# Layer 2's first 256 columns in one part, and attention's buffers in one pool in the order in which they come free

## The chip, the cores and the metric

One NeuronCore of a Trainium2 chip runs the program. The metric is the device time of one execution in microseconds (us); lower is better.

## What is computed

Linear attention with a feature map, and on its output a soft mixture of experts. Shapes: q, k, v are 8 batches x 8 heads x 576 tokens x 64; the feature map has 128 features; the tokens x are 4608 x 512; there are 8 experts with 4 slots each, of width 1024. All is float32.

```python
def phi(x):
    proj = np.einsum('bhsd,df->bhsf', x, w_phi)
    proj = proj - np.max(np.abs(proj), axis=-1, keepdims=True)
    return np.concatenate([np.exp(proj), np.exp(-proj)], axis=-1)
q_p, k_p = (phi(q), phi(k))
kv = np.einsum('bhsf,bhsd->bhfd', k_p, v)
z = np.sum(k_p, axis=2)
num = np.einsum('bhsf,bhfd->bhsd', q_p, kv)
den = np.einsum('bhsf,bhf->bhs', q_p, z)[..., None] + 1e-06
...
logits = x @ phi                                   # 4608 x 32
d = softmax(logits, over tokens); slot_input = d.T @ x
slot_out[e] = np.maximum(slot_input[e] @ w1[e], 0.0) @ w2[e]
c = softmax(logits, over slots); out = c @ slot_out
```

## The kernel before

**Stages.** Attention runs in a pipeline over blocks of four tiles of 128 tokens. A planner (`Plan`) holds tasks by kind, each with what must have been done before it; `ORDER`, a string with one letter a task, says in which order they are recorded, and so in which order each engine finds its instructions. Two letters matter here: `I` (late), the load of one weight, and `Q` (close), the closing of a pool of attention's buffers. After attention come the token softmax and the slots' inputs (acc), then layer 1 (`layer1`, L930: si times w1 into hp), `hidden` (relu on ACT, a 32 x 32 transpose on DVE, giving sh), layer 2 (`layer2`, L995) and the outputs.

**Weights.** There are 64 loads (tiles wt0 to wt63) of 512 KB on SP's queue: 32 of w1, then 16 for the first 256 columns of w2 (wt32 to wt47), then 16 for the last 256 (wt48 to wt63). On chip they lie in 53 slots of 4096 bytes a partition. Slots 0 to 29 are free from the start. Slots 30 to 52 (`LATE`) lie where attention's buffers lie: a load into one waits until the users of those buffers (`over(j)`) are done: vt and vs (values), kf and qf (features of k and q), kvs, un, xs, xT, xc, xn and wk. The last 11 loads go into slots whose w1 part layer 1 has read. A load also waits for the landing of the one five before it, and SP takes its queue strictly in order. The buffers lie in six pools (`LAYOUT`, `LIFO`: x, v, q, u, t, c), and a pool's slots can be loaded once this pool is closed.

**Layer 2 and outputs.** `layer2(q, e)` multiplies the hidden values of expert e by 128 columns (`COLS`) of w2: eight matmuls of 32 rows, in four column slices that run side by side; a part q is complete after eight of these, and there are four parts. Then `slots(q)` copies it from PSUM (yp) to yt on DVE, `slots2(q)` sums the four slices and repeats them with `rep` on PE (psy) and copies that on ACT, and `outputs(q, g)`, three per part, multiplies by c (four pso matmuls of 384 columns), copies with DVE and ACT and issues two output DMAs of 384 KB on SP. `TAIL` orders this: L a call of `layer2`, s `slots`, r `slots2`, O `outputs`, P the second `hidden`.

```python
TAIL = "LPLLLLLLLLsrLLOLOLLLLsOrLLLOLLOLLLsOLrLLOLLOLLLsOrOOO"
```

All 24 outputs stand behind the last weight on SP. PE finds its instructions in the order of `TAIL`, and so do DVE and ACT.

Of the kernel before, what the change touches and what calls it, by code (L numbers as in the profile page):

```python
# [22 lines left out]
NCH = NT // CH  # L23
# [26 lines left out]
BASE, TOP = 8064, 226816  # L50
LAYOUT = (("x", "xs", (4096,) * 3, 1), ("v", "vt", (2624,) * 2, 0), ("v", "kf", (4096,) * 3, 0), ("v", "vs", (2624,) * 2, 0), ("q", "wd", (512,), 0),
          ("q", "qf", (4096,) * 3, 0), ("q", "kvs", (1056,) * 2, 0), ("u", "un", (2368,) * 2, 0), ("t", "xT", (4096,) * 3, 0), ("t", "wk", (4096,), 0),
          ("c", "xc", (8192,), 0), ("c", "xn", (8192,), 0), ("c", "xc", (8192,), 1))
LIFO = "xvqutc"


def regions():

    at, got = TOP - sum(sum(n) for _, _, n, _ in LAYOUT), []
    for k, name, sizes, first in LAYOUT:  # L60
        for i, n in enumerate(sizes):
            got.append((at, at + n, k, (name, (i + first) % max(len(sizes), first + 1))))
            at += n
    return got
# [4 lines left out]
PAD = REGIONS[0][0] - BASE - 4096 * FIRST  # L69
NSLOT = [FIRST] + [(max(b for _, b, x, _ in REGIONS if x == k) - BASE - PAD) // 4096 for k in LIFO]  # L70


def over(j):

    a = BASE + PAD + 4096 * j
    return [name for lo, hi, _, name in REGIONS if lo < a + 4096 and a < hi]

# [4 lines left out]
class Plan:  # L82
# [56 lines left out]
    "jAAknoowacwydfgccqhodgmmjfhillablsmpqzirrdktvrnjjfmkowvgjavwwAccbsxnyzofAhhrAAxdknilltviwmmrrjmgjvJpAqsrwfkAnhkx"  # L139
    "mnvooowdgtvwrvwcdccQMNikndjjlloIIIyzgjmmAAAfflrvhprimwhygjrzimqspQIIIIkknAAltRSRnSRoovIqrvTTRRwwvwAknrrrQIIyszST"  # L140
    "SSIItvAAwyvwUvTTzyzoAARRRSSXwyTTzSTY4AXRZYZSA0>UXQIRXYYSTTZWW002225536W36>553557799>QIII88868+8QIIW+++/=/=IIIIIO"
    "OP<!!!POP!")

COLS = 128
TAIL = "LPLLLLLLLLsrLLOLOLLLLsOrLLLOLLOLLLsOLrLLOLLOLLLsOrOOO"


@with_exitstack  # L150
def tile_kernel(ctx: ExitStack, tc, xT, vv, w, phi, phi4, w1, w2, cst, out):
# [24 lines left out]

    def pool(k, name, **kw):
        return stacks[k].enter_context(tc.tile_pool(name=name, **kw))

    area = {k: pool(k, k + "p", bufs=1, side="right") for k in reversed(LIFO)}  # L180

    def place_in(name, i, shape, as_=None):

        k = next(k for k, n, *_ in LAYOUT if n == name)
        return area[k].tile(shape, F32, tag=f"{name}{i}", name=as_ or name)

    for lo, hi, _, (name, i) in REGIONS:
        place_in(name, i, [128, (hi - lo) // 4], "lay")
# [687 lines left out]

    def close(k):
        stacks[k].close()
# [3 lines left out]
    every = {"x": [("proj", NB)], "v": [("kpos_exp", NB - 1), ("kvmm", len(pieces) - 1), ("vals", len(pieces) - 1), ("kvcopy", NU - 1)], "q": [("num", NK - 1)],  # L882
             "u": [("divide", (NU - 1, 2))], "t": [("zlog", c) for c in range(NCH)] + [("zcw", c) for c in range(NCH)] + [("zdt", c) for c in range(NCH)], "c": [("zsum", 4)]}
    users = {("xs", 1): [("proj", NB - 3)], ("xs", 2): [("proj", NB - 1)], ("xs", 0): [("proj", NB)], ("wd", 0): [("proj", NB)]}
# [59 lines left out]

    for i, k in enumerate(LIFO):
        add("close", i, None, 0.0, lambda k=k: close(k), after=every[k] + ([("close", i - 1)] if i else [("weight", FIRST - 1)]))
    for i, j in enumerate(LATE):
        add("late", i, SP, 1.3, lambda: load_w(1), after=[x for name in over(j) for x in users[name]], order=[("close", sum(j >= n for n in NSLOT) - 1)])
    with tc.manual_schedule(engines={SP, PE, ACT, DVE, POOL}):
# [39 lines left out]

        def layer2(q, e):  # L990
            if q not in yp:
                yp[q] = numbered(hb[0][q % 2], [128, COLS], "yp")
            for c in range(FC):
                g, o = 32 * (c % 4), c % 4 * DH + q % 2 * COLS
                nc.tensor.matmul(yp[q][g:g + 32], sh[e // 4][:, FC * (e % 4) + c],  # L995
                                 wt[NE * KC + (q // 2 * NE + e) * 2 + c // 4][:, o:o + COLS],
                                 start=(e == 0 and c < 4), stop=(e == NE - 1 and c >= 4), skip_group_check=True)

        yt = slot(spare[2], "yt").rearrange("p (i q c) -> p i q c", i=2, q=4)

        def slots(q):
            nc.vector.tensor_copy(yt[:, 0, q], yp[q])

        def slots2(q):
            ps = bank([128, COLS], "psy")
            for j in range(4):
                nc.tensor.matmul(ps[32 * j:32 * j + 32], rep, yt[:, 0, q], start=True, stop=True, skip_group_check=True)
            return nc.scalar.copy(yt[:, 1, q], ps).ins

        def outputs(q, g):  # L1010

            ps = [bank([128, TRI * 128], "pso") for _ in range(G)]
            c = ct[g // 2][:, g % 2 * TRI * 128:(g % 2 + 1) * TRI * 128]
            for j in range(G):
                rows = slice(32 * j, 32 * j + 32)
                nc.tensor.matmul(ps[j], yt[rows, 1, q], c[rows], start=True, stop=True)  # L1016
# [12 lines left out]
        cturn(1, 6, 9)  # L1029
        l2 = iter([(q, e) for q in range(4) for e in range(NE)])  # L1030
        done, outs = 0, []
        for step in TAIL:
            if step == "L":
                layer2(*next(l2))
            elif step == "P":
                hidden(1)
                cps += hb[1]
            elif step == "O":
                outputs(*outs.pop(0))
            elif step == "s":  # L1040
# [47 lines left out]
```

## Time and profile before

| | us |
|---|---|
| three timed runs | 309.3, 311.18, 311.4 (median 311.18) |
| the profiled execution's own time | 310.53 |
| its span, first to last instruction | 308.6 |
| around the span | 1.9 |

The profiled execution is one run. Its durations make up the working; its own time is 0.65 us under the median of the timed runs, which lie 2.1 us apart. PE is TensorE, DVE VectorE, ACT ScalarE, POOL GpSimd, and SPq the queue of SyncE, which issues the loads and outputs. A float32 matmul shows as two records on PE and two weight loads on PEld.

### The profile page before, as it was taken

Reading aid. Unit: us, or ns where it says so; the run is one execution under the profiler, and the core shown is the slowest. Engines: PE = TensorE matmul, PEld = TensorE weight load, DVE = VectorE, ACT = ScalarE, POOL = GpSimd, SP = SyncE. Lnnn points to the kernel's source line nnn. Section 1 sums busy time; section 2 is a strip of 40 time slices with the busy share of each in tenths; the row PEclk is TensorE's granted clock in tenths of the full one; section 3 lists DMA queues with packets and bytes.
Section 4 is the critical chain, followed back from the end, with each engine's and each line's share of the span. In section 5 each row is a group of like instructions: output and inputs, shape, how many; then the busy total and the mean of one; then the engine's idle time right before and its main releaser. Section 6 shows DMA issues by size and latency. Waiting matters only on the chain.

```text
span 308.6 us, 16094 instructions
## 1 busy us (share of the span) xinstructions
PE 296.2 (96%) x6805; PEld 251.5 (82%) x6805; DVE 243.3 (79%) x703; ACT 223.9 (73%) x658; POOL 159.2 (52%) x333
## 2 busy tenths in 40 slices
PE   8999999999999999999999999999999999999880
PEld 4999999998879999988799999897998853376550
DVE  0689888999898999889988989689887958624361
ACT  3999799888597998967978888887987560223351
POOL 1548677874367676953577776546788302000000
PEclk9999999999999999999999999999999999999996
DMA  7646564653339188435779888268487999999897
GB/s 244 215 153 189 179 191 149 240 181 127 99 91 329 52 261 285 163 113 185 252 230 331 259 266 293 55 206 295 118 262 267 355 340 374 411 407 408 349 359 309
DMA packets 23398, 74.01 MB, mean 240 GB/s; under 512 B 2592, under 2 KB 2976, under 8 KB 23328
## 3 DMA queue, kind: packets, MB, share of 16 engines
q1 hardware_dynamic: 23184, 72.94, 68.3%
q8 instruction: 53, 0.87, 1.1%
q14 instruction: 17, 0.14, 0.1%
q10 hardware_dynamic: 144, 0.07, 0.1%
HBM read 63.55 MB, written 9.44 MB: 237 GB/s over the span
## 4 chain that ended last, share of the span: by engine, by line
PE 90%; DVE 4%; issue 2%; DMA 1%; ACT 1%; POOL 0%; DVEq 0%; ACTq 0%
PE kvp L363 24%; PE psn L416 21%; PE psk L317 15%; PE psq L315 7%; PE yp L995 5%; PE hp L930 4%; PE pso L1016 3%; PE psq L496 3%; PE pss L556 2%; DMA wd<-w 1%; PE psw L229 1%; PE pss L659 1%; PE psk L309 1%; DVE un L432 1%; PE psl L506 1%
## 5 line engine op out<-in xcount | busy, mean ns | idle before, releaser
L336 POOL TENSOR_TENSOR vs<-vt,call 128x520 f32<-128x520 f32 (+3 forms) x128 | 91.2, 732 | 40.0 <-ACT call L325 17.8
L363 PE MATMUL kvp<-vs,kf 128*64 128x65 f32 (+1 forms) x2304 | 86.6, 229 | 0.1
L363 PEld LDWEIGHTS kvp<-vs,kf 128*64 128x64 f32 x2304 | 79.1, 138 | 5.4 <-issue 1.5
L416 PE MATMUL psn<-kvs,qf 128*64 128x65 f32 x2304 | 78.1, 222 | 0.2 <-issue 0.2
L416 PEld LDWEIGHTS psn<-kvs,qf 128*64 128x64 f32 x2304 | 72.7, 138 | 3.4 <-issue 1.3
L317 PE MATMUL psk<-wd,xs 64*128 64x128 f32 x560 | 70.9, 279 | 0.0
L315 PE MATMUL psq<-xs,wd 64*128 64x512 f32 x140 | 70.6, 616 | 0.4 <-PE psk L317 0.2
L317 PEld LDWEIGHTS psk<-wd,xs 64*128 64x128 f32 x560 | 63.9, 187 | 0.0
L321 DVE TENSOR_REDUCE call<-psk 128x4 f32<-128x512 f32 x72 | 47.6, 674 | 12.6 <-PE psk L309 5.9
L378 DVE TRANSPOSE_TENSOR_REDUCE call<-psq 128x16 f32<-128x512 f32 x72 | 48.9, 696 | 4.8 <-PE psk L317 4.1
L347 ACT ACTIVATE kf<-psk 128x512 f32<-128x512 f32 x72 | 42.1, 592 | 13.6 <-PE kvp L363 5.3
L462 POOL TENSOR_TENSOR xc<-un,dn 128x256 f32<-128x256 f32 x63 | 38.6, 616 | 14.3 <-DVE dn L447 9.9
L383 ACT ACTIVATE qf<-psq 128x512 f32<-128x512 f32 x72 | 42.0, 591 | 5.2 <-PE psk L317 2.4
L350 ACT ACTIVATE kf<-psk 128x512 f32<-128x512 f32 x72 | 42.4, 596 | 0.4 <-DVE call L321 0.4
L386 ACT ACTIVATE qf<-psq 128x512 f32<-128x512 f32 x72 | 42.4, 595 | 0.0
L427 DVE TENSOR_TENSOR un<-psn,eq 128x195 f32<-128x195 f32 x96 | 32.6, 348 | 6.4 <-PE psn L416 3.2
L432 DVE TENSOR_TENSOR un<-psn,un 128x195 f32<-128x195 f32 x96 | 32.2, 352 | 1.4
L394 ACT ACTIVATE call<-call 32x36 f32<-32x36 f32 x128 | 29.4, 229 | 5.0 <-DVE call L378 1.7
L400 DVE TENSOR_REDUCE eq<-call 32x9 f32<-32x36 f32 x128 | 25.9, 203 | 1.9 <-ACT call L394 0.6
L315 PEld LDWEIGHTS psq<-xs,wd 64*128 64x128 f32 x140 | 20.8, 186 | 5.7 <-issue 1.6
L1020 ACT COPY o<-pso 128x384 f32<-128x384 f32 x24 | 10.2, 484 | 15.3 <-PE pso L1016 15.3
L1020 DVE COPY o<-pso 128x384 f32<-128x384 f32 x24 | 12.1, 552 | 11.5 <-PE pso L1016 11.5
(125 smaller groups left out, 288.5 us busy)
## 6 DMA issues: line engine op xcount, KB each, us to landing
wt<-w SPq DMA_DIRECT2D x64, 512.0 KB, 6.2
xs<-xT SPq DMA_DIRECT2D x34, 512.0 KB, 4.8
vt<-vv SPq DMA_DIRECT2D x32, 325.0 KB, 3.1
out<-o SPq DMA_DIRECT2D x24, 384.0 KB, 3.9
xs<-xT SPq DMA_DIRECT2D x4, 256.0 KB, 3.9
phq<-phi SPq DMA_DIRECT2D x1, 256.0 KB, 2.7
cs<-cst SPq DMA_DIRECT2D x1, 81.0 KB, 3.4
wd<-w ACTq DMA_DIRECT2D x1, 64.0 KB, 3.0
```

Source lines behind the costliest of these rows:

```text
L315: nc.tensor.matmul(qx[b - 2], wd[qh], x[qh], start=True, stop=True)
L317: nc.tensor.matmul(kx[b][:, i], x[kh, i], wd[kh], start=True, stop=True)
L321: nc.vector.tensor_reduce(km[b][:, 2], kx[b], axis=AX, op=ALU.max, apply_absolute_value=True)
L336: nc.gpsimd.tensor_tensor(vs[b][:, :, place(b, u, t, o):place(b, u, t, o) + n], v[:, t + o:t + o + n].unsqueeze(1).broadcast_to([128, 2, n ...
L347: nc.scalar.activation(kf[b][:, 1], kx[b], AF.Exp, scale=-1.0)
L350: nc.scalar.activation(kf[b][:, 0], kx[b], AF.Exp)
L363: nc.tensor.matmul(ps[f:f + FE // 2, pn, o:o + m], kf[b][:, pn, NT * u + t - 4 * b, f:f + FE // 2], v2[:, pn, at:at + m], start=(t == 0 an ...
L378: nc.vector.tensor_reduce(mts.rearrange("p r j -> p j r")[:, o:o + 4], qx[b].rearrange("p j (r t) -> p (j r) t", t=32), axis=AX, op=ALU.ma ...
L383: nc.scalar.activation(qf[b][:, 0], qx[b], AF.Exp)
L386: nc.scalar.activation(qf[b][:, 1], qx[b], AF.Exp, scale=-1.0)
L416: nc.tensor.matmul(ps[64 * f:64 * f + 64, j, pn], q2[:, pn, 64 * f:64 * f + 64], kv[:, pn, b2], start=True, stop=True)
L462: (divider(u) if c == 2 else nc.gpsimd).tensor_tensor(x[:, :, h * D:(h + 1) * D], un[u][:, a:b, 0:64], dn[u][:, a:b].unsqueeze(2).broadcas ...
```

## The change

The buffers of attention go into one pool (`area`), closed once, and lie in a new order; all 23 late loads are recorded after this close (in `ORDER` the `I`s before it move behind it, the other letters keep their order). Each load still waits for the users of the buffers that its slot lies on. Layer 2 has three parts, of 256, 128 and 128 columns, in place of four of 128.

```diff
-LAYOUT = (("x", "xs", (4096,) * 3, 1), ("v", "vt", (2624,) * 2, 0), ("v", "kf", (4096,) * 3, 0), ("v", "vs", (2624,) * 2, 0), ("q", "wd", (512,), 0),
-          ("q", "qf", (4096,) * 3, 0), ("q", "kvs", (1056,) * 2, 0), ("u", "un", (2368,) * 2, 0), ("t", "xT", (4096,) * 3, 0), ("t", "wk", (4096,), 0),
-          ("c", "xc", (8192,), 0), ("c", "xn", (8192,), 0), ("c", "xc", (8192,), 1))
-LIFO = "xvqutc"
+LAYOUT = "xs1 vt0 xs2 xs0 wd0 kf0 kf1 vs0 vt1 kf2 vs1 kvs0 qf0 qf1 kvs1 qf2 un0 un1 xT0 xT1 xT2 xc0 wk0 xn0 xc1".split()
...
-COLS = 128
-TAIL = "LPLLLLLLLLsrLLOLOLLLLsOrLLLOLLOLLLsOLrLLOLLOLLLsOrOOO"
+PARTS = (0, 256), (256, 128), (384, 128)
+TAIL = "LLLPLLLLLsrLOLOLLLOLLOLLsOOLLrLOLLLLsOOrOOO"
...
-    area = {k: pool(k, k + "p", bufs=1, side="right") for k in reversed(LIFO)}
+    area = held.enter_context(tc.tile_pool(name="area", bufs=1, side="right"))
...
-    for i, k in enumerate(LIFO):
-        add("close", i, None, 0.0, lambda k=k: close(k), after=every[k] + ([("close", i - 1)] if i else [("weight", FIRST - 1)]))
+    add("close", 0, None, 0.0, close, after=sorted({x for name in users for x in users[name]} | {("kpos_exp", NB - 1), ("kvcopy", NU - 1), ("weight", FIRST - 1)}, key=str))
     for i, j in enumerate(LATE):
-        add("late", i, SP, 1.3, lambda: load_w(1), after=[x for name in over(j) for x in users[name]], order=[("close", sum(j >= n for n in NSLOT) - 1)])
+        add("late", i, SP, 1.3, lambda: load_w(1), after=[x for name in over(j) for x in users[name]], order=[("close", 0)])
...
-        def layer2(q, e):
-            if q not in yp:
-                yp[q] = numbered(hb[0][q % 2], [128, COLS], "yp")
+        def layer2(p, e):
+            at, n = PARTS[p]
+            if p not in yp:
+                yp[p] = numbered(hb[0][p % 2], [128, n], "yp")
             for c in range(FC):
...
-        def slots(q):
-            nc.vector.tensor_copy(yt[:, 0, q], yp[q])
+        def slots(p):
+            at, n = PARTS[p]
+            nc.vector.tensor_copy(yt[:, 0, at:at + n], yp[p])
...
-                nc.tensor.matmul(ps[32 * j:32 * j + 32], rep, yt[:, 0, q], start=True, stop=True, skip_group_check=True)
-            return nc.scalar.copy(yt[:, 1, q], ps).ins
+                nc.tensor.matmul(ps[32 * j:32 * j + 32], rep, yt[:, 0, at:at + n], start=True, stop=True, skip_group_check=True)
+            nc.scalar.copy(yt[:, 1, at:at + n], ps)
...
             else:
                 slots2(done)
-                outs += [(done, g) for g in range(3)]
+                at, n = PARTS[done]
+                outs += [(q, g) for q in range(at // 128, (at + n) // 128) for g in range(3)]
                 done += 1
```

On PE, around the end of layer 2's first part, the program before reads as follows. The numbers on wt are counters of the program: 5724 and 5726 are wt46 and wt47, 5216 to 5480 wt32 to wt38; x4 are the four slices.

```order
L995 MATMUL yp<-wt_5724,sh 32x128 x4
L995 MATMUL yp<-wt_5726,sh 32x128 x4
L995 MATMUL yp<-wt_5216,sh 32x128 x4
L995 MATMUL yp<-wt_5350,sh 32x128 x4
L1007 MATMUL psy<-yt,cs 32x128 x4
L995 MATMUL yp<-wt_5352,sh 32x128 x4
L995 MATMUL yp<-wt_5354,sh 32x128 x4
L995 MATMUL yp<-wt_5356,sh 32x128 x4
L995 MATMUL yp<-wt_5390,sh 32x128 x4
L1016 MATMUL pso<-ct,yt 128x384 x4
L995 MATMUL yp<-wt_5480,sh 32x128 x4
```

After the change the same place reads as follows; 5687 to 5691 are wt45 to wt47, 5723 to 5729 wt48 to wt51.

```order
L986 MATMUL yp<-wt_5687,sh 32x256 x4
L986 MATMUL yp<-wt_5689,sh 32x256 x4
L986 MATMUL yp<-wt_5691,sh 32x256 x4
L1000 MATMUL psy<-yt,cs 32x256 x4
L986 MATMUL yp<-wt_5723,sh 32x128 x4
L986 MATMUL yp<-wt_5725,sh 32x128 x4
L1009 MATMUL pso<-ct,yt 128x384 x4
L986 MATMUL yp<-wt_5727,sh 32x128 x4
L986 MATMUL yp<-wt_5729,sh 32x128 x4
L1009 MATMUL pso<-ct,yt 128x384 x4
```

The psy matmuls, which read what DVE copies from the finished part, now follow right behind its last matmul, and one call of `layer2` instead of two stands between psy and the first pso.

On SP, the weight loads from wt33 (5350) on read as follows in the program before; DMAHW is the landing of an earlier load, Pool and PE the releases of buffers.

```order
L194 DMA wt_5350<-w 128x1024 [waits DMAHW6_49,Pool_49]
L194 DMA wt_5352<-w 128x1024 [waits DMAHW7_49,PE_49,Activation_49]
L194 DMA wt_5354<-w 128x1024 [waits DMAHW0_49,PE_49,Activation_49]
L194 DMA wt_5356<-w 128x1024 [waits DMAHW1_49,PE_49,Activation_49]
L194 DMA wt_5390<-w 128x1024 [waits DMAHW2_49]
```

And after the change, again from wt33 (5663) on:

```order
L187 DMA wt_5663<-w 128x1024 [waits DMAHW6_49,PE_49,Activation_49]
L187 DMA wt_5665<-w 128x1024 [waits DMAHW7_49,PE_49,Activation_49]
L187 DMA wt_5667<-w 128x1024 [waits DMAHW0_49,Pool_49]
L187 DMA wt_5669<-w 128x1024 [waits DMAHW1_49,Pool_49]
L187 DMA wt_5671<-w 128x1024 [waits DMAHW2_49,PE_49,Activation_49]
```

The load that waits for POOL's last `vals` stands three places later, and two that wait for PE and ACT (kf) stand ahead of it. In the same way wt46 waited for DVE's call (`zcw`, L632) before, and wt48 does after.

## Rows read from the trace of the kernel before

**Rows 1.** The page, parts 1 and 3: busy engines; instruction queue (packets, MB, share)

```profile
PE 296.2 (96%) x6805; PEld 251.5 (82%) x6805; DVE 243.3 (79%) x703; ACT 223.9 (73%) x658; POOL 159.2 (52%) x333
q8 instruction: 53, 0.87, 1.1%
```

**Rows 2.** Stretches: length; busy (instructions) of PE, PEld, DVE, ACT, POOL; PEclk, DMA share, GB/s

```profile
220.00:240.00 20.00, 20.00 (x498) 18.74 (x496) 15.81 (x46) 16.89 (x48) 15.90 (x34) 1.00 0.77 248
...
280.79:287.53 6.74, 5.25 (x128) 3.50 (x128) 2.34 (x5) 1.89 (x5) 0.00 (x0) 1.00 1.03 407
288.00:296.00 8.00, 8.00 (x201) 5.37 (x197) 4.17 (x9) 3.56 (x9) 0.00 (x0) 1.00 0.81 320
```

**Rows 3.** Single DMAs by tile, SP: issue, and time to landing under it

```profile
L194 SPq DMA_DIRECT2D wt<-w x1: 328/328/328, 276.7 to 276.7; - x1
...
DMA to landing us min/median/max: 6.3/6.3/6.3
...
L1021 SPq DMA_DIRECT2D out<-o x1: 347/347/347, 278.1 to 278.1; - x1
...
DMA to landing us min/median/max: 5.9/5.9/5.9
...
L1021 SPq DMA_DIRECT2D out<-o x1: 332/332/332, 291.4 to 291.4; - x1
...
DMA to landing us min/median/max: 2.6/2.6/2.6
...
L1021 SPq DMA_DIRECT2D out<-o x1: 332/332/332, 295.8 to 295.8; - x1
...
DMA to landing us min/median/max: 3.4/3.4/3.4
...
L1021 SPq DMA_DIRECT2D out<-o x1: 891/891/891, 303.6 to 303.6; - x1
...
DMA to landing us min/median/max: 4.0/4.0/4.0
```

**Rows 4.** The chain that ended last: start us, us, what

```profile
257.60 13.73 PE hp L930 x128
271.34 3.93 PE yp L995 x144
...
280.18 0.62 issue
...
286.06 1.49 issue
...
288.47 1.45 PE yp L995 x48
...
290.78 0.57 PE yp L995 x16
...
293.30 1.01 PE yp L995 x32
```

**Rows 5.** Who waited for whom on SP's queue, 224 to 262 us: total, times, longest

```profile
SPq L194 <- POOL vs L336: 2.7, 1, 2.7
SPq L194 <- DVE call L632: 2.5, 1, 2.5
```

**Rows 6.** Groups by form, 270 to 305 us: count, busy us, mean ns, idle before

```profile
L1020 DVE COPY o<-pso 128x384 f32<-128x384 f32 x24 | 12.1, 552 | 11.5 <-PE pso L1016 11.5
L1020 ACT COPY o<-pso 128x384 f32<-128x384 f32 x24 | 10.2, 484 | 15.3 <-PE pso L1016 15.3
L1007 PE MATMUL psy<-yt,cs 128*32 128x128 f32 x32 | 1.7, 282 | 0.0
...
L1002 DVE COPY yt<-yp 128x128 f32<-128x128 f32 x4 | 1.2, 292 | 4.9 <-PE yp L995 4.9
L1008 ACT COPY yt<-psy 128x128 f32<-128x128 f32 x4 | 1.1, 275 | 3.6 <-PE psy L1007 3.6
```

**Rows 7.** Timeline of PE: start us, us

```profile
276.48 0.93 PE L1016 MATMUL pso<-ct,yt 32*128 32x384 f32 x8
```

More of the change, by code (lines that the diff above doesn't have):

```diff
@@ L50 @@
 BASE, TOP = 8064, 226816
-LAYOUT = (("x", "xs", (4096,) * 3, 1), ("v", "vt", (2624,) * 2, 0), ("v", "kf", (4096,) * 3, 0), ("v", "vs", (2624,) * 2, 0), ("q", "wd", (512,), 0),
-          ("q", "qf", (4096,) * 3, 0), ("q", "kvs", (1056,) * 2, 0), ("u", "un", (2368,) * 2, 0), ("t", "xT", (4096,) * 3, 0), ("t", "wk", (4096,), 0),
-          ("c", "xc", (8192,), 0), ("c", "xn", (8192,), 0), ("c", "xc", (8192,), 1))
-LIFO = "xvqutc"
+SIZE = {"xs": 4096, "vt": 2624, "kf": 4096, "vs": 2624, "wd": 512, "qf": 4096, "kvs": 1056, "un": 2368, "xT": 4096, "wk": 4096, "xc": 8192, "xn": 8192}
+LAYOUT = "xs1 vt0 xs2 xs0 wd0 kf0 kf1 vs0 vt1 kf2 vs1 kvs0 qf0 qf1 kvs1 qf2 un0 un1 xT0 xT1 xT2 xc0 wk0 xn0 xc1".split()
 def regions():
[L59 to L63, printed above, removed]
+    at, got = TOP - sum(SIZE[x[:-1]] for x in LAYOUT), []
+    for x in LAYOUT:
+        got.append((at, at + SIZE[x[:-1]], (x[:-1], int(x[-1]))))
+        at = got[-1][1]
     return got
@@ L69 @@
 PAD = REGIONS[0][0] - BASE - 4096 * FIRST
-NSLOT = [FIRST] + [(max(b for _, b, x, _ in REGIONS if x == k) - BASE - PAD) // 4096 for k in LIFO]
+NSLOT = [FIRST, (REGIONS[-1][1] - BASE - PAD) // 4096]
 def over(j):
     a = BASE + PAD + 4096 * j
-    return [name for lo, hi, _, name in REGIONS if lo < a + 4096 and a < hi]
+    return [name for lo, hi, name in REGIONS if lo < a + 4096 and a < hi]
 LATE = list(range(FIRST, NSLOT[-1]))
@@ L164, in tile_kernel @@
     psum = ctx.enter_context(tc.tile_pool(name="psum", bufs=1, space=PSUM))
-    stacks = {k: ExitStack() for k in ("x", "c", "t", "u", "q", "v")}
+    held = ExitStack()
     def numbered(i, shape, name):
@@ L175, in bank3 @@
         return numbered(plan.held["pb", label][0], shape, name)
[L177 to L180 removed]
+    area = held.enter_context(tc.tile_pool(name="area", bufs=1, side="right"))
     def place_in(name, i, shape, as_=None):
[L184 to L187 removed]
+        return area.tile(shape, F32, tag=f"{name}{i}", name=as_ or name)
+    for lo, hi, (name, i) in REGIONS:
         place_in(name, i, [128, (hi - lo) // 4], "lay")
@@ L875, in tile_kernel, with close @@
         add("weight", i, SP, 1.3, lambda: load_w(1), after=[("consts", 0)] + [("quarters", (NBP - 2, KC - 1))] * (i == FIRST - 1), at=1000)
-    def close(k):
-        stacks[k].close()
+    def close():
+        held.close()
         opened()
     last_kv = {b: ("kvmm", max(i for i in range(len(pieces)) if pieces[i][0] == b)) for b in range(NB)}
-    every = {"x": [("proj", NB)], "v": [("kpos_exp", NB - 1), ("kvmm", len(pieces) - 1), ("vals", len(pieces) - 1), ("kvcopy", NU - 1)], "q": [("num", NK - 1)],
-             "u": [("divide", (NU - 1, 2))], "t": [("zlog", c) for c in range(NCH)] + [("zcw", c) for c in range(NCH)] + [("zdt", c) for c in range(NCH)], "c": [("zsum", 4)]}
     users = {("xs", 1): [("proj", NB - 3)], ("xs", 2): [("proj", NB - 1)], ("xs", 0): [("proj", NB)], ("wd", 0): [("proj", NB)]}
@@ L1015, in outputs @@
                 rows = slice(32 * j, 32 * j + 32)
-                nc.tensor.matmul(ps[j], yt[rows, 1, q], c[rows], start=True, stop=True)
+                nc.tensor.matmul(ps[j], yt[rows, 1, q * 128:q * 128 + 128], c[rows], start=True, stop=True)
             for k in range(2):
@@ L1029, in tile_kernel @@
         cturn(1, 6, 9)
-        l2 = iter([(q, e) for q in range(4) for e in range(NE)])
+        l2 = iter([(p, e) for p in range(len(PARTS)) for e in range(NE)])
         done, outs = 0, []
@@ L1041, in tile_kernel @@
                 slots(done)
-                if done > 1:
+                if done > 0:
                     cps.append(hb[0][done % 2])
```

19 lines of the change are left out of this document (10 added, 9 removed).

## The prediction

> **What bounds the kernel now.** I read the page first: PE is busy for 96% of the span and the other engines for less [rows 1], an average over two very different stages. So I went on to the table of stretches: up to 240 us PE is never idle; in the last 25 us the DMA is full, at 407 GB/s and a share of 1.03, and PE has holes [rows 2]. The landings say what this means for the end. The last of the 64 weight loads lands at 276.7 + 6.3 = 283.0 us, the first output at 278.1 + 5.9 = 284.0, the last at 303.6 + 4.0 = 307.6 [rows 3]. So outputs follow the weights without a break, and the end is the 24 outputs. The output issued at 295.8 lands at 299.2, and nine more follow it to 307.6: 0.935 us each. Without a pause, 23 of these after 284.0 would end at 305.5; the pauses between outputs are 2.1 us. The stretch 288 to 296 shows them: DMA share 0.81 [rows 2].
>
> Why do outputs pause? The chain gives two idle times of PE in this phase that no engine ended: "issue" 0.62 us at 280.18 and 1.49 us at 286.06 [rows 4]. The stretch from the end of the one to the end of the other holds 128 matmuls and 128 weight loads, exactly 256 instructions [rows 2]. The page's q8 moved 53 instruction packets, 0.87 MB, while PE ran 13,610 instructions [rows 1]: 257 a packet. I read both stops as PE waiting for its own code, brought by the DMA rings that the weights and outputs fill. A block seems to need up to 6.74 us between two starts when these are full.
>
> By the Trainium skill (Runtime: NRT & Kernel Launch, Instruction fetch mechanics) code comes in blocks of 256 instructions, and the cost of crossing a block is mostly hidden. The trace agrees on the 256, not on "hidden" here, where it shows 2.1 us; were the rule right, the two stops would have another cause: the fifth rival below.
>
> **The change: loads.** The planner's letters for all other tasks keep their order, so the five engines do the same up to layer 2; only SP's queue differs. Before, wt33 stands behind the last `vals` (POOL vs, 2.7 us of waiting at the queue's head), wt46 behind DVE's call (2.5 us) [rows 5]; what stands behind them waits too. After, loads whose buffers PE frees come first (kvp), the POOL ones three places later, and call's two later. The stream can come forward by nothing (if the next release decides) up to 2.7 + 2.5 = 5.2 us. I take 2.4, near the middle, since other releases between the two keep their places: last weight at 280.6, not 283.0. This is hidden whatever it is: the weights of layer 2's first half are long there, and an output needs PE's result first. If that cover were gone, it would be the 2.4 us.
>
> **The change: PE up to the first output.** Layer 2 begins at 271.34 in the chain, and layer 1 before it takes 13.73 us for 128 matmul records of 512 columns, so a group of eight records (four slices) takes 0.858 us and one of 256 columns 0.429 [rows 4]. The first part now is 16 such groups, 6.86 us, and ends at 278.2. Before it was 16 groups of 128, 3.93 us for 144 records, 0.218 each, followed by two more of the next part to cover DVE's copy. Per column nothing is gained: two old parts are 32 x 0.218 = 6.98, so 0.1 us.
>
> By the Trainium skill (TensorEngine Tiling, Instruction Overhead) every matmul has about 60 cycles of overhead; 64 fewer would then save an estimated 1.6 us, and the sum would be 2.1 us faster, all that pauses leave. The trace disagrees: 0.218 against half of 0.429 leaves 0.004 us a group.
>
> Now no multiplication stands between the end of the part and its `rep` matmuls (psy), so PE waits for DVE. The copies grow from 128 to 256 columns. DVE takes 292 ns for 128 columns, 552 for 384; ACT 275 and 484 [rows 6]. Between them I take 0.42 and 0.36. With 0.06 us at each handing over: DVE 278.26 to 278.68; psy at 278.74, done 0.65 later (1.7 us for four of 128 columns, 0.43 each [rows 6], and 0.22 for the second 128); ACT 279.45 to 279.81; the first pso at 279.87. Bounds for the three: 0.4 below (nothing grows) and 0.3 above (copies as for 384). Before, the first pso began at 276.48 [rows 7]. So PE is 3.4 us later with its first result. That is the cost: half a layer before the first output, not a quarter.
>
> **The change: outputs.** A step of pso takes PE 0.86 us (from 288.47 + 1.45 to 290.78), one, two or three `layer2` calls 0.57, 1.01 or 1.45 [rows 4], a fourth 0.44 more. From pso to the issue of the first of its two outputs it took 278.1 - 276.48 = 1.6 [rows 3, 7], and an output with no queue ahead lands 2.6 us after issue (the one issued at 291.4) [rows 3]. So the first output now lands at 279.87 + 1.6 + 2.6 = 284.1, as before, although the weights are done at 280.6: the lead is lost to a DMA gap.
>
> From there six output steps are ready at once, not three. PE's steps (0.1 more where a pso waits for copied banks): second 281.3, third 283.7, fourth 285.6, fifth 287.5, sixth 288.4. DVE's and ACT's copies take about 1.1 us a step and keep up. Then two calls, psy at 290.9, ACT's copy, seventh pso at 291.7; four calls, eighth pso at 294.4. The DMA needs 1.87 us for a step. A step's first output lands 1.87 after that of the step before, or 4.2 after its pso if that is later: the third is 0.1 late, the seventh 0.5, the eighth 0.9. The eighth's first output lands at 298.6; it is the 15th of 24, and 9 x 0.935 later the last lands: 307.0. The four left are ready early.
>
> PE's code: 64 matmuls fewer are 256 instructions, one block less. The first part is one whole block of 7 us, where it was 3.9. The next starts at psy (278.8); the one after in the middle of the pair after the third step (285.1), 6.3 us later; the next before the seventh step (291.7), 6.6 later. With the 6.74 of before these would stop PE for 0.4 and 0.1 us; with less loaded rings for nothing. I take nothing, and 0.5 as the upper end.
>
> **The sum.** Last landing 307.0 against 307.63: 0.6 to 0.7 us less, in the profiled execution's own time 310.53 - 0.7 = 309.8. Pauses fall from 2.1 to 1.5. Copies can add 0.3 and code 0.5; the copies can take 0.4 off. The three timed runs are 309.3, 311.18 and 311.4; with the profiled one their middle is 310.9, so I say 310.2.
>
> **Rivals.**
> First, the pauses vanish altogether, because copies and banks cost less than I add and PE never stops: 284.1 + 23 x 0.935 = 305.6, 2.0 us less: 308.8. For it: half the instructions in the first part. Against it: the four calls ahead of the eighth pso are in the program.
>
> Second, outputs begin earlier as well, using up to 1.3 us of the weights' lead of 2.4: 3.3 us less, 307.5. It needs PE to reach psy sooner than its columns allow, or the end of attention to come sooner because less waits on DMA. Nothing in the chain before 257.6 waits for a weight, so this is the weaker one.
>
> Third, slower: the fuller stream from 233 to 257 us slows PE's code at the end of attention. Between 220 and 240 PE went through 498 + 496 instructions in 20 us [rows 2], a block in 5.2 us. If a block needs 6.74 there, as in the full stretch, PE stops 1.6 us at each of two blocks, 3.1 us. All from there to the first output is now PE's chain without slack (before there was slack, as outputs waited for weights), so the end comes 3.1 - 0.7 = 2.4 us later: 313.3. It beats the gain from 0.7 us of stops on. Against it: the DMA's share from 220 to 240 is 0.77 [rows 2], and PE has no hole in it (20.00 of 20.00 us), so a block comes within 5.2 us at that load.
>
> Fourth, the change doesn't do what it says: the new order of buffers isn't the order of release, and the stream comes no earlier. By the steps above this costs nothing while the last weight lands by 283: 310.2 as well.
>
> Fifth, PE's two stops are no code, and stay with half the instructions: the eighth pso comes 0.62 + 1.49 = 2.1 us later and with it the end, 312.3. Against it: the 256 instructions between them. By the Trainium skill's rule above this would be the case.
>
> **How the numbers follow.** 1% of 311.2 is 3.1 us, about what a measurement of this kernel tells from no change. Forecast and fourth rival together 0.48 (310.2); first rival 0.18 (308.8, within 1%, though scatter of the runs may take it below 308.1); second 0.13 (307.5, faster); third 0.13 (313.3, slower by 0.7%, beyond 314.3 only with a third stop); fifth 0.08 (312.3). Faster: the second, and a quarter of the first, 0.17. Slower: half of the third and a little for what I don't see, 0.1. Same: 0.73. The range takes in the first and most of the second and the third: 307.7 to 313.2.
>
> **What would show it.** Right: the last weight lands about 280 to 281; the first output is issued near 281.5 and lands near 284.1, with a dip in the DMA's share between; no "issue" of 0.5 us or more on PE after 271 us; small pauses before the 13th and 15th output; the last landing near 307. Wrong: layer 1 not starting near 257.6 (third rival); first output issued before 280.5 or outputs landing with no pause (first and second); new stops of PE 256 instructions apart.

## The result, and the profile after

| | before | after |
|---|---|---|
| median of 20 runs each | 309.67 us (308.39 to 314.05) | 311.51 us (309.74 to 314.35) |
| profiled execution: own time, span | 310.53, 308.6 | 312.23, 310.3 |

After over before is 1.0056, 95% interval [1.0033, 1.0079]: the change costs about 1.7 us (1.0 to 2.4). A second measurement (e7, below) gave 1.0026 [1.0001, 1.0051]. I had forecast 0.7 us less. The change lies within the 1% that I called "same", but the sign is wrong. That the median lies within my range is partly luck: I had started from 310.9 us, 1.2 above the median of the kernel before.

First the page of the kernel after, parts 1 and 3, beside [rows 1].

```profile
PE 296.8 (96%) x6669; PEld 249.3 (80%) x6669; DVE 243.0 (78%) x702; ACT 223.4 (72%) x657; POOL 158.8 (51%) x333
...
q8 instruction: 52, 0.85, 1.1%
```

PE has 136 matmul records and 136 weight loads less, one packet of code less. The busy times don't tell a slower kernel from a faster one.

The stretches that answer to [rows 2], with the same columns:

```profile
220.00:240.00 20.00, 19.36 (x499) 18.13 (x496) 14.89 (x45) 16.32 (x48) 16.37 (x34) 1.00 0.81 274
...
288.00:296.00 8.00, 8.00 (x180) 5.45 (x184) 4.31 (x10) 3.71 (x9) 0.00 (x0) 1.00 1.01 390
```

From 288 to 296 us the DMA share rose from 0.81 to 1.01: the idle time that I had found there is gone. From 220 to 240 PE now has a hole of 0.64 us that it didn't have.

The chain that ended last, beside [rows 4] (start us, us, what), from the end of attention to the first output:

```profile
237.74 0.64 issue
...
259.02 13.73 PE hp L921 x128
272.75 6.95 PE yp L986 x128
...
279.73 0.43 DVE yt L994
...
280.21 0.68 PE psy L1000 x8
...
280.91 0.38 ACT yt L1001
...
281.34 0.93 PE pso L1009 x8
```

Layer 1 starts at 259.02 in place of 257.60, takes the same 13.73 us, and the first pso comes 22.3 us after it. No "issue" of more than 0.1 us follows up to 299 us: PE stops no more for code after layer 1.

Single DMAs, beside [rows 3] (issue, and time to landing under it): the last weight, the first four outputs, the last output.

```profile
L187 SPq DMA_DIRECT2D wt<-w x1: 327/327/327, 278.6 to 278.6; - x1
...
DMA to landing us min/median/max: 6.3/6.3/6.3
...
L1014 SPq DMA_DIRECT2D out<-o x4: 332/353/599, 282.9 to 284.8; - x4
...
DMA to landing us min/median/max: 2.9/3.3/5.4
...
L1014 SPq DMA_DIRECT2D out<-o x1: 930/930/930, 304.8 to 304.8; - x1
...
DMA to landing us min/median/max: 4.5/4.5/4.5
```

The last weight lands at 284.8 (before 283.0), the first output is issued at 282.9 and lands at 285.8 (before 278.1 and 284.0), the last lands at 309.3 (before 307.6). The first three outputs need 2.9 to 3.4 us; the fourth, issued at 284.8, needs 5.4.

That fourth output led me to what landings do not show. Stretches of 2 us of the kernel before (columns as in [rows 2]; the last two are DMA share and GB/s):

```profile
282.00:284.00 2.00, 2.00 (x64) 1.47 (x56) 1.05 (x3) 1.03 (x3) 0.00 (x0) 1.00 1.04 413
...
288.00:290.00 2.00, 2.00 (x60) 1.40 (x56) 1.03 (x3) 0.86 (x2) 0.00 (x0) 1.00 0.67 262
...
294.00:296.00 2.00, 2.00 (x53) 1.26 (x49) 1.15 (x3) 0.99 (x3) 0.00 (x0) 1.00 0.72 278
```

And of the kernel after:

```profile
280.00:282.00 2.00, 1.74 (x32) 0.95 (x32) 0.15 (x1) 0.37 (x1) 0.00 (x0) 1.00 1.04 412
282.00:284.00 2.00, 2.00 (x39) 1.06 (x39) 1.31 (x3) 1.10 (x3) 0.00 (x0) 1.00 0.52 203
284.00:286.00 2.00, 2.00 (x56) 1.30 (x45) 0.74 (x2) 0.62 (x2) 0.00 (x0) 1.00 1.02 400
```

Before, the DMA is full across the change from weights to outputs and idles in part later, at 288 and 294. After, it is idle for half of 282 to 284, while the last weight still is on its way to its landing at 284.8, and full after that. The trace has, for every transfer, the times at which its 16 parts were done; the last of them is the landing. The first part of the last weight was done at 282.6 us, half of them by 283.2 and the last at 284.8, and the first output was issued at 282.9. So engines stood without work while one of them still carried the weight. By the Trainium skill (DMA: Bandwidth & Descriptors, Why a DMA increments its semaphore by 16 and not by 1) a DMA runs on up to 16 engines that finish independently, and only when all have finished is the data there; these times, and the share of 0.52 under a weight in flight, agree with that.

So the saving is there, and so is a new loss of much the same size, one step earlier. Whether that is the whole of it the experiments had to tell.

### The profile page after: what moved, and what is told of

The parts are those of the page before. It is cut to its first block, busy times and chain, and to the rows that moved or that the text cites. A ratio compares the mean times of both kernels' runs of the same rounds, so it can differ in the third digit from the quotient of the medians.

```text
span 310.3 us, 15822 instructions
## 1 busy us (share of the span) xinstructions
PE 296.8 (96%) x6669; PEld 249.3 (80%) x6669; DVE 243.0 (78%) x702; ACT 223.4 (72%) x657; POOL 158.8 (51%) x333
## 4 chain that ended last, share of the span: by engine, by line
PE 91%; ACT 3%; DVE 2%; issue 1%; DVEq 0%; POOL 0%; ACTq 0%; POOLq 0%
PE kvp L356 24%; PE psn L409 22%; PE psk L310 14%; PE psq L308 7%; PE yp L986 5%; PE hp L921 4%; PE pso L1009 3%; PE psq L489 3%; PE pss L549 2%; PE psx L830 2%; PE psw L222 1%; DVE call L314 1%; PE pss L652 1%; PE psl L467 1%; PE psk L302 1%
## 5 line engine op out<-in xcount | busy, mean ns | idle before, releaser
L329 POOL TENSOR_TENSOR vs<-vt,call 128x520 f32<-128x520 f32 (+3 forms) x128 | 91.1, 730 | 40.2 <-ACT call L318 25.4
L393 DVE TENSOR_REDUCE eq<-call 32x9 f32<-32x36 f32 x128 | 25.9, 203 | 1.9 <-ACT call L387 0.6
L317 ACT ACTIVATE call<-call 128x4 f32<-128x4 f32 x72 | 15.0, 209 | 7.8 <-DVE call L314 7.1
L478 DVE STREAM_TRANSPOSE xT<-xc 128x256 f32<-128x256 f32 x48 | 17.8, 414 | 1.9 <-PE psq L489 1.9
```

The source lines that it names most:

```text
L329: nc.gpsimd.tensor_tensor(vs[b][:, :, place(b, u, t, o):place(b, u, t, o) + n], v[:, t + o:t + o + n].unsqueeze(1).broadcast_to([128, 2, n ...
```

## The experiments

All times from layer 1 on are counted from its first matmul, in the timeline 257.42 us before and 258.83 after (the step of the chain begins 0.2 later). The table collects what is read in every profile; the shares are those of three stretches, 20 to 30, 30 to 40 and 40 to 49 us after that matmul. A full DMA shows 1.03.

| kernel | layer 1 begins | first output issued, after that | last landing, after that | DMA share | ratio to before, interval |
|---|---|---|---|---|---|
| before | 257.42 | 20.6 | 50.2 | 1.03, 0.86, 0.97 | 1 |
| before again (e8) | 258.29 | 20.7 | 50.6 | 1.03, 0.89, 1.01 | |
| before, third (e12) | 256.55 | 20.7 | 49.3 | 1.00, 0.95, 0.97 | |
| e1: pool alone | 256.76 | 20.6 | 49.6 | 1.02, 0.89, 0.93 | 1.0006 [0.9973, 1.0039] |
| e6: before, longer | 258.12 | 20.7 | 50.9 | 1.02, 0.98, 0.93 | 1.0022 [0.9991, 1.0054] |
| after | 258.83 | 24.1 | 50.5 | 0.92, 0.98, 1.01 | 1.0056 [1.0033, 1.0079] |
| after again (e7) | 257.62 | 24.1 | 50.4 | 0.85, 0.97, 1.02 | 1.0026 [1.0001, 1.0051] |
| after, third (e13) | 256.41 | 24.1 | 50.4 | 0.90, 0.97, 1.02 | |
| after, fourth (e14) | 260.00 | 24.1 | 50.4 | 0.89, 0.97, 1.02 | |
| e2: part alone | 258.82 | 24.1 | 50.4 | 0.90, 0.97, 1.01 | 1.0051 [1.0025, 1.0076] |
| e5: after, longer | 257.69 | 24.1 | 51.3 | 0.88, 0.97, 1.02 | 1.0087 [1.0053, 1.012] |
| e11: first part in halves | 258.32 | 23.6 | 50.2 | 0.83, 0.96, 1.01 | 1.0055 [1.002, 1.009] |
| e9: 128, 128, 256 | 258.88 | 20.6 | 51.3 | 0.97, 0.74, 1.01 | 1.0038 [1.0009, 1.0067] |
| e10: four parts, late | 258.56 | 26.7 | 54.5 | 0.69, 0.95, 0.99 | 1.0125 [1.009, 1.0161] |

e8, e12, e13 and e14 are one timed run each, the profiled one: 311.65, 308.93, 309.76 and 313.29 us.

The expectations name their theories; the letters A to D in the text below are those of the runs from e5 on: A, attention is slower after the change because of the place or length of PE's code; B, the late first output lets the DMA run dry; C, what attention differs by is chance; D, merging as such costs.

**Which half of the change costs (e1, e2).** e1 is the changed kernel with layer 2 as before:

```diff
-PARTS = (0, 256), (256, 128), (384, 128)
-TAIL = "LLLPLLLLLsrLOLOLLLOLLOLLsOOLLrLOLLLLsOOrOOO"
+PARTS = (0, 128), (128, 128), (256, 128), (384, 128)
+TAIL = "LPLLLLLLLLsrLLOLOLLLLsOrLLLOLLOLLLsOLrLLOLLOLLLsOrOOO"
...
-                if done > 0:
+                if done > len(PARTS) - 3:
```

> The buffers' new order and the single pool, with layer 2 in four parts of 128 columns and their old sequence. Theory S (the fuller stream of loads holds up PE's code at the end of attention, and from there all is late): layer 1 starts at 258.4 to 259 instead of 257.6, a stop of PE of 0.6 us or more near 238, last weight at 284 to 285, time ratio to before 1.003 to 1.008, as for the whole change. Theory P (the cost is the longer way to the first output): the stream's lead is used here, last weight at 281, outputs right behind it, ratio about 0.993.

e2 is the kernel before, six pools and all, with the changed kernel's parts, `TAIL` and functions of layer 2:

```diff
-COLS = 128
-TAIL = "LPLLLLLLLLsrLLOLOLLLLsOrLLLOLLOLLLsOLrLLOLLOLLLsOrOOO"
+PARTS = (0, 256), (256, 128), (384, 128)
+TAIL = "LLLPLLLLLsrLOLOLLLOLLOLLsOOLLrLOLLLLsOOrOOO"
...
-                if done > 1:
+                if done > 0:
```

> Layer 2 in parts of 256, 128 and 128 columns with the new sequence, and the old six pools and load order. Theory S: no loss, layer 1 starts at 257.6, first pso at 279.9, first output lands at 284.1 as before, fewer pauses behind it, ratio 0.997 to 1.000. Theory P: the whole loss is here, ratio 1.004 to 1.008.

Measured: 310.16 us and ratio 1.0006 [0.9973, 1.0039] for the pool alone, 311.41 us and 1.0051 [1.0025, 1.0076] for the part alone. The loss goes with layer 2's new parts and their order; the new order of buffers neither costs nor saves anything that can be told. S, which put the loss on the loads, falls; the saving that P expected of e1 (0.993) did not come either.

**Fewer loads in flight (e3, e4).** In the kernel after and in the one before:

```diff
-LATER = 5
+LATER = 3
```

> The whole change, with at most three late loads in flight instead of five (LATER 3), so that PE's code has a shorter queue before it. Theory S: the stop near 238 is gone, layer 1 starts by 258.0, ratio to before 1.001 or less. Theory P: first output as late as with the whole change, ratio 1.004 to 1.008; more if three in flight do not fill the DMA.

> The kernel before with three late loads in flight instead of five. If PE's two stops near 280 and 286 are a wait for code behind the loads: they shrink from 0.62 and 1.49 us to under 0.5 each, pauses between outputs fall, ratio 0.993 to 0.999. If they are something else: they stay, ratio 1.000, or above 1.005 where three in flight do not fill the DMA (last weight after 284).

Measured: 318.69 us, 1.0321 [1.027, 1.0372], and 320.53 us, 1.0338 [1.0302, 1.0374]. The 20 us from the first matmul of layer 1, in e3 and then in e4 (columns as in [rows 2]):

```profile
259.75:279.75 20.00, 20.00 (x261) 7.94 (x258) 11.18 (x37) 3.68 (x7) 1.85 (x3) 1.00 0.88 311
```

```profile
256.54:276.54 20.00, 20.00 (x340) 9.38 (x338) 11.47 (x38) 3.95 (x8) 1.85 (x3) 1.00 0.84 296
```

With three loads of 512 KB in flight the DMA moves 311 and 296 GB/s in place of 410 in the same stretch of the kernel after. Both kernels now wait for weights at the end, and the last landing is 59.6 and 59.7 us after layer 1 begins: where weights set the end, the cut of layer 2 makes no difference. The edit acts on the late loads alone, from 225 us on. PE's longest stops in e3, of 1.44 us at 126 and 0.41 at 174, lie ahead of that, so the run says nothing of them; the stop near 238 is missing, as it is in most profiles of the new order (below). In e4 both stops of [rows 4] are gone: PE runs without a pause from 273.9 to 285.6 us, as I had expected if they are waits for code behind the loads. Only then does it wait for weights.

**Is attention slower after the change (e5 to e8, e12 to e14)?** In the profiles 1.4 us of the loss lay ahead of layer 1, where both kernels have the same instructions on PE. e5 puts 68 small matmuls, whose result nobody uses, behind the last pso of the kernel after, so that PE's program is as long as before; e6 does it to the kernel before (with `yt[:, 0, 0, 0:16]`).

```diff
+        ps = bank([128, 16], "psd")
+        for i in range(68):
+            nc.tensor.matmul(ps[32 * (i % 4):32 * (i % 4) + 32], rep, yt[:, 0, 0:16], start=True, stop=True, skip_group_check=True)
```

> The changed kernel with 68 small matmuls (272 PE instructions) behind the last pso, so that PE's program is as long as before the change; they run beside the drain of the outputs. Their result is used by nobody. Theory A (the loss is PE's attention meeting more stops for code, and these hang on the length or place of PE's program): ratio 1.000, layer 1 begins near 257 us. Theory B (the loss is in the tail: the first output is late and the DMA runs dry near 282 us): ratio 1.005 as for the changed kernel, layer 1 wherever chance puts it, last landing less start of layer 1 near 50.5 us. Theory C (the stops are chance, the medians differ by the tail alone): as B, and the layer 1 starts of the repeated profiles of both kernels overlap.

> The kernel before with the same 68 matmuls behind its last pso; their result is used by nobody. Theory A: if length as such matters, the time moves by 0.3% or more and layer 1 begins a microsecond or more away from 257; Theories B and C: ratio 1.000 (0.998 to 1.002), last landing less start of layer 1 50.2 us.

Measured: 312.63 us, 1.0087 [1.0053, 1.012], and 310.39 us, 1.0022 [0.9991, 1.0054]. A falls in this form: the longer program is not back at 1.000, and against e6, which carries the same matmuls, e5 takes 1.0065 times as long. The added matmuls weren't free: in e5 the last landing comes 51.3 us after layer 1 begins, in e6 50.9, each about 0.9 later than without them (50.4, and a mean of 50.0 before). B and C had expected 50.5 and 50.2. The trace shows what they cost. From layer 1 on PE's code comes in six packets of 16 KB in e5 and in five in the kernel after. The additional one runs from 44.55 to 45.51 us after layer 1 begins, the 18th output still lands where it does in the kernel after (44.9 and 44.8), and the 19th lands 0.97 us later (46.7 and 45.75). The median of the 16 parts of the last output is done at 49.6 in both kernels: only some parts are late.

The other four are the two kernels unchanged, for more profiles.

> The changed kernel once more, for a second profile. Theory A: layer 1 begins near 258.8 us again, ratio 1.005. Theory C: layer 1 begins anywhere between 256.5 and 259.5, while the last landing less start of layer 1 stays within 0.3 us of 50.5; ratio 1.005.

> The kernel before once more, for a second profile. Theory A: layer 1 begins near 257 us. Theory C: anywhere between 256.5 and 259.5, last landing less start of layer 1 near 50.2 us.

> The kernel before, third profile. Theory A' (attention is slower after the change): layer 1 begins between 256.5 and 258.3. Theory C (scatter): anywhere from 256.5 to 259.5. Last landing 50.2 to 50.6 after that.

> The changed kernel, third profile. Theory A': layer 1 begins after 258. Theory C: anywhere from 256.5 to 259.5. Last landing 50.4 to 50.5 after that.

> The changed kernel, fourth profile. Theory A': layer 1 begins after 258 us. Theory C: anywhere from 256.5 to 259.5. Last landing 50.4 to 50.5 after that.

Layer 1's step in the chains of e12, e13 and e14, each in a fence of its own:

```profile
256.73 13.74 PE hp L930 x128
```

```profile
256.60 13.73 PE hp L921 x128
```

```profile
260.18 13.73 PE hp L921 x128
```

The kernel before starts layer 1 at 256.6 to 258.3 us in three profiles, the kernel after at 256.4 to 260.0 in four; the earliest of all is one of after. So the 1.4 us of the first pair of profiles can't be read as the change's: one pair is within the scatter (C). What differs from profile to profile are for the most part stops of PE of 0.1 to 1.7 us, at multiples of 256 instructions from one another and at changing places. Whether their mean differs too is not settled: the means of the starts are 257.4 and 258.2, from three and four profiles with standard deviations of 0.9 and 1.6. Taken over more runs, the eight profiles with the wide first part (after, e2, e3, e5, e7, e11, e13, e14) begin layer 1 at 258.4 on average, the six with the four parts in their old order (before, e1, e4, e6, e8, e12) at 257.3: 1.1 us apart, two standard errors. Most of it is there by 206 us, before the late loads begin, on instructions that are the same. So a slower attention (A in a form other than length) is neither shown nor excluded.

From layer 1 on the picture is steady for the kernel after: the last landing comes 50.4 to 50.5 us later in all four profiles, and in e2. For the kernel before it varies, 49.3 to 50.6, mean 50.0, as its stops for code after layer 1 do (0.62 and 1.49 us in [rows 4]; 0.83 and 0.94 in e8's chain; 0.83 and 0.39 in e12's).

**Is it the late first output, or the merging (e9, e10)?** e9 merges the other half of the columns, so that the first output is early again:

```diff
-PARTS = (0, 256), (256, 128), (384, 128)
-TAIL = "LLLPLLLLLsrLOLOLLLOLLOLLsOOLLrLOLLLLsOOrOOO"
+PARTS = (0, 128), (128, 128), (256, 256)
+TAIL = "LPLLLLLLLLsrLLOLOLLLLsOrLLLOLLOLLLsOrOOOOOO"
```

> The changed kernel with its three parts the other way round: 128, 128 and then 256 columns, so that the first output needs 8 calls of layer 2 again while PE's program keeps the 256 instructions less. Theory B (the late first output empties the DMA for 1.0 to 1.7 us, which eats what the shorter program saves later): no dip of the DMA near 282 us (start of layer 1 + 24), first output issued 20.6 us after layer 1 begins; one wait before the 13th output, whose part needs all of layer 2 (pso at layer 1 + 34.8 without stops); last landing less start of layer 1 49.3, about 1 us less than both kernels, ratio to before 0.995 to 1.000. Theory D (merging as such costs, wherever it stands): last landing less start of layer 1 50.4 or more, ratio 1.003 or more.

e10 is e1 with the first output as late as in the kernel after, and nothing merged:

```diff
-TAIL = "LPLLLLLLLLsrLLOLOLLLLsOrLLLOLLOLLLsOLrLLOLLOLLLsOrOOO"
+TAIL = "LLLPLLLLLLsLLrLLLLLsrLOLOLLLOLLOLLsOOLLrLOLLLLsOOrOOO"
```

> Four parts of 128 columns in the changed kernel's pool, but with all 16 calls of the first two parts ahead of the first output, as late as in the changed kernel; behind them the order of the changed kernel. Theory B: the DMA runs dry near layer 1 + 24 for 1 to 1.7 us as in the changed kernel, though nothing is merged; last landing less start of layer 1 50.5 to 51.5, ratio to before 1.003 to 1.009, against 1.0006 for the same four parts with an early first output. Theory D: 50.2 or less and ratio 1.000.

Measured: e9 310.84 us, 1.0038 [1.0009, 1.0067]; e10 313.67 us, 1.0125 [1.009, 1.0161]. Stretches of e9, and after them its PE timeline around the 13th output's pso (start us, us, instruction, idle time before it and what ended it):

```profile
282.00:284.00 2.00, 1.68 (x36) 0.94 (x36) 0.29 (x1) 0.00 (x0) 0.00 (x0) 1.00 1.02 409
...
288.00:290.00 2.00, 2.00 (x36) 1.09 (x32) 0.89 (x2) 0.77 (x2) 0.00 (x0) 1.00 0.70 263
290.00:292.00 2.00, 2.00 (x36) 0.94 (x32) 1.02 (x2) 0.86 (x2) 0.00 (x0) 1.00 0.66 258
...
294.00:296.00 2.00, 1.32 (x20) 0.64 (x20) 1.02 (x2) 1.14 (x3) 0.00 (x0) 1.00 0.23 88
```

```profile
294.08 0.64 PE L1000 MATMUL psy<-yt,cs 128*32 128x256 f32 x8
295.40 0.93 PE L1009 MATMUL pso<-ct,yt 32*128 32x384 f32 x8 [0.68 <-ACT yt L1001]
```

B's first half held: with an early first output the dip behind the weights is gone. My number did not, and the result, 51.3 us and 1.0038, is what D had expected: I had the 13th output's pso 34.8 us after layer 1 begins, and it came after 36.5, because PE also stopped and waited for copies; the DMA idled for 2.9 us there, and the end came 0.9 us later than in the kernel after, not 1.1 earlier. The idle time had moved again, to where the wide part now stands.

Stretches of e10, and two rows of its PE timeline:

```profile
280.00:282.00 2.00, 0.47 (x12) 0.20 (x14) 0.29 (x1) 0.00 (x0) 0.00 (x0) 1.00 1.00 399
282.00:284.00 2.00, 2.00 (x32) 1.07 (x32) 0.00 (x0) 0.27 (x1) 0.00 (x0) 0.63 0.44 168
284.00:286.00 2.00, 2.00 (x24) 1.05 (x24) 1.02 (x2) 0.86 (x2) 0.00 (x0) 0.52 0.03 10
```

```profile
281.12 0.43 PE L986 MATMUL yp<-wt,sh 128*32 128x128 f32 x8 [1.40 <-issue]
...
282.94 1.66 PE L1009 MATMUL pso<-ct,yt 32*128 32x384 f32 x8
```

Nothing is merged in e10, and yet the DMA runs dry before the first output, for 3 us, and the kernel is 1.2% slower than before, against 0.06% for the same four parts in e1. So lateness costs without any merging, and D's 1.000 for e10 fails. That merging as such costs nothing is not shown, since e9 came out as D expected; e9's wait before the 13th output is my explanation of it. e10 came out beyond B's bound (1.009), since a stop for code of 1.4 us and a slower clock (below) made the first output later still, 26.7 us after layer 1 begins in place of 24.1.

**Does the first output count one to one (e11)?** In the changed kernel, copies and psy in pieces of 128 columns, and no call of layer 2 ahead of the first pso:

```diff
-TAIL = "LLLPLLLLLsrLOLOLLLOLLOLLsOOLLrLOLLLLsOOrOOO"
+TAIL = "LLLPLLLLLsrOLLOLLLOLLOLLsOOLLrLOLLLLsOOrOOO"
...
-            nc.vector.tensor_copy(yt[:, 0, at:at + n], yp[p])
+            for i in range(0, n, 128):
+                nc.vector.tensor_copy(yt[:, 0, at + i:at + i + 128], yp[p][:, i:i + 128])
...
-            ps = bank([128, n], "psy")
+            for i in range(at, at + n, 128):
+                ps = bank([128, 128], "psy")
```

> The changed kernel, but the copies of a finished part and its psy go in pieces of 128 columns, and no call of layer 2 stands between psy and the first pso: the first pso should begin 0.6 us earlier, 21.9 us after layer 1 begins instead of 22.5. Theory B (the first output's time counts one to one, since the DMA is empty before it): first output issued 23.5 after layer 1 begins instead of 24.1, the DMA's idle time between 20 and 30 us after it 0.6 less, last landing 49.8 instead of 50.45 us after layer 1 begins. Rival (the later steps of PE set the end, not the first output): last landing stays at 50.4 or more.

Measured: 311.45 us, 1.0055 [1.002, 1.009]. PE's timeline at the first pso, and the stretch in which the DMA runs out a second time:

```profile
280.37 0.93 PE L1011 MATMUL pso<-ct,yt 32*128 32x384 f32 x8 [0.17 <-ACT yt L1003]
```

```profile
296.00:298.00 2.00, 1.15 (x24) 0.28 (x16) 1.95 (x4) 1.80 (x5) 0.00 (x0) 1.00 0.79 313
```

The first pso came 22.05 us after layer 1 begins, 0.46 earlier than in the kernel after (0.6 expected), and the last landing 50.2, 0.25 earlier (0.65 expected). The idle time between 20 and 30 us did not shrink, as I had expected it to (share 0.83), because the last weight landed earlier in this run as well, 24.6 us after layer 1 begins (25.5 to 26.0 in the four profiles of after). Part of the gain was given back at 296 to 298, share 0.79 against 0.85 in the kernel after: later steps had not moved. 50.2 is neither B's 49.8 nor the rival's 50.4, and one profile and a ratio equal to that of after cannot tell between them.

No version measured is faster than the kernel before; e1 is equal to it.

## Why the prediction was wrong

**The first rows (what bounds the kernel).** Right: the tail is the DMA's, and PE's two "issue" stops were stops for code. Both end 1.4 us after a packet of 16 KB of queue q8 (instruction) has ended, and so it is everywhere: in the sixteen traces PE has 34 such stops of 0.25 us or more between 15 us and the last outputs, and every one ends 1.3 to 1.8 us after the end of such a packet. No profile of the changed kernel has one after layer 1, and with it the fifth rival falls: had the stops been something else, they would have stayed. By the Trainium skill (Runtime: NRT & Kernel Launch, Instruction fetch mechanics) crossing a block of 256 instructions is mostly hidden; stops of 0.6 to 1.5 us in the kernel before and of 1.40 in e10 say that here it is not. Incomplete: I read from landings that outputs follow weights "without a break", and landings show the slowest part of a transfer only. The same holds for my 2.1 us of pauses: 1.5 of them lie at the 12th output, which has one part at 39.0 us after layer 1, while the other fifteen are done by 37.4.

**The loads' stream.** I took 2.4 us, from bounds of 0 and 5.2. It was near 0: counted from layer 1, the last weight lands at 25.6, 26.3 and 25.8 us in the three profiles before, at 26.0, 25.5, 25.6 and 25.9 in the four after, and at 25.0 in e1. The waits of [rows 5] are gone as I said, and these took their place on SP's queue (224 to 262 us):

```profile
SPq L187 <- PE psn L409: 6.3, 4, 3.9
SPq L187 <- PE kvp L356: 4.1, 3, 2.2
...
SPq L187 <- DVE xc L455: 3.6, 1, 3.6
```

The lower bound, "if the next release decides", was the right one. It was costed at nothing, and e1 and e2 (1.0006 with the new order alone, 1.0051 without it) show nothing that it is worth.

**PE up to the first output.** Right to 0.05 us: forecast 279.87 - 257.60 = 22.27 us from the chain's layer 1 to the first pso, measured 281.34 - 259.02 = 22.32. The part took 6.95 us (6.86 forecast), so wide calls save nothing per column; the copies, beside [rows 6] (mean ns after the busy time):

```profile
L994 DVE COPY yt<-yp 128x256 f32<-128x256 f32 x1 | 0.4, 424 | 5.5 <-PE yp L986 5.5
L1001 ACT COPY yt<-psy 128x256 f32<-128x256 f32 x1 | 0.4, 372 | 7.4 <-PE psy L1000 7.4
```

They are 0.42 and 0.37, where I had taken 0.42 and 0.36. Against 6.98 us for the same columns in 32 groups before, 6.95 is no gain from 64 matmuls fewer. By the Trainium skill's rule (TensorEngine Tiling (Array Packing), Instruction Overhead) they would have saved an estimated 1.6 us; the trace disagrees.

**The outputs: the step that failed.** The sentence was: "So the first output now lands at 279.87 + 1.6 + 2.6 = 284.1, as before". That landing was right (26.8 us after the chain's layer 1 against 26.5 forecast). What I built on it was wrong: 0.935 us an output from there, with pauses of 0.1, 0.5 and 0.9 before the third, seventh and eighth step. Before the change, when the first output landed, it had been issued 5.9 us earlier and the fourth 3.6 us earlier, and the DMA had never been empty: its engines were well into the next three. After it, the first had been issued 2.9 us earlier, the fourth 1.0, and the DMA had just filled again. The same landing stood for about a microsecond of work less. I had put this gap at nothing. The times at which the 16 parts of an output were done show it, counted from layer 1: the median part of the first output was done at 25.4, 26.0 and 24.9 us in the three profiles before and at 26.3 in all four after, 0.9 later on average, though the last part came no later. In stretches: the share from 20 to 30 us fell from 1.00 to 1.03 down to 0.85 to 0.92, a loss of 1.1 to 1.8 us; from 30 to 40 us it rose from 0.86 to 0.95 up to 0.97 or 0.98, a gain of up to 1.2. My sum held the gain and not the loss. Counted against 1.03 and over all three stretches, the DMA idles 1.6 to 2.2 us before and 1.8 to 2.5 after. On the median part loss and gain cancel: the last output's was done at 49.95, 49.98 and 49.14 before and at 49.63 to 49.65 after.

What is left is in the slowest part. It comes 0.2 to 0.6 us behind the median at the last output before, and 0.7 to 0.9 after. It fell behind at the fourth output, which landed 2.5 to 2.7 us after the third and not 0.93 (and by another 0.4 at the eleventh). That is not the idle DMA: 15 of its 16 parts were done by 29.6 to 29.8 us after layer 1 began, and one at 31.3, in all four profiles. In each a packet of PE's code begins at 29.1 to 29.2, which is 288.0 us in the first profile of the kernel after; the row of queue q8 from 287 to 289 us (packets, MB, share of 16 engines):

```profile
q8 instruction: 1, 0.02, 2.9%
```

2.9% of 16 engines' 2 us are 0.93 us of one engine. In e11 the packet comes at 26.7 us, and there it is the third output that has one part 1.4 us behind the rest; in e10 it comes at 29.9, takes 1.9 us, and the third output has one part 2.5 us behind. That the packet holds up the late part is inferred from these times; the trace doesn't name the engine of a packet.

Of the pauses that I had forecast, that before the eighth step is there, 0.55 us on the median part where I had 0.9 (share 0.85 at 296 to 298); those before the third and the seventh are not.

**The sum.** From layer 1 to the last landing I had 0.6 to 0.7 us less. Measured: 0.27 more between the two first profiles; 50.4 against 50.0, 0.4 more, over four and three. The timed runs say 1.7 more. So about a quarter of the measured loss is seen in the tail, and as the three tails before lie between 49.3 and 50.6 even this is not clear of their scatter. The rest lies in attention, whose 1.1 us (above) would suffice but are not shown, or in tails of the kernel before that are shorter than my three profiles of it, and stays open.

**Rivals.** The third named the place of PE's hole in the first profile: 0.64 us at 237.74, and layer 1 not at 257.6. One profile would have made it the winner. But stops near there occur in 3 of 10 profiles with the new pool (they put layer 1 0.4 to 0.9 us later) and hardly in the six with the old one (0.2 in e2), e1 with the same stream measures 1.0006, and e2 loses as much without it. It may be worth some 0.2 us on average; it is not the cause of the loss that e2 has too. The mechanism that the tail shows, a later first output that leaves DMA engines without work, stood in my own text as "the lead is lost to a DMA gap", with no price.

## What to carry to other kernels

Where one stream of transfers follows another, price the seam by the DMA's share in short stretches, not by landings: a landing is that of the slowest part, and a last transfer can be in flight while half of the DMA is idle. A landing that comes late need not be idle time either: look at what else, code for one, the engines carried. A step that makes work coarser moves idle time rather than removing it; ask what each consumer has in its queue at the moment when the first result comes. And before a difference of half a per cent is put down to a place in one profile, take several profiles and count from a mark that both kernels share.

## What the runs showed of the hardware that I had not expected

- Identical attention code started layer 1 anywhere from 256.4 to 260.0 us. The stops that make this up lie 256 PE instructions apart or multiples of that, last 0.1 to 1.7 us, and come at other places in each profile. All 34 of 0.25 us or more end 1.3 to 1.8 us after a 16 KB packet of code has ended.
- Three loads of 512 KB in flight don't fill the DMA: 296 to 311 GB/s against 410 with five, and 3.2 to 3.4% of the time (e3, e4).
- In e10 the granted clock of TensorE fell to 0.63 and 0.52 (the lower level, 1.2 GHz, for most of 284 to 286) right after 2 us in which PE was busy for 0.47; a step of pso began there that took 1.66 us in place of 0.93. In the kernel after, where PE's waits are shorter, the clock stayed at 1.00 up to 300 us.
- A packet of 16 KB of code takes 0.9 to 1.9 us, and one part of an output then in flight is done 1.4 to 2.5 us behind the other fifteen (fourth output of the kernel after, third of e10 and e11). One more such packet, for 68 small matmuls behind the last pso, comes with a last landing about 0.9 us later (e5, e6).
